# Attention and gated experts on one core: v summed a block early, one fetch moved behind a pair, three casts and one guess moved

## The chip, the core and the metric

The kernel runs on one core of a Trainium2 chip. A core has five engines that run side by side, each through its own instructions in order: TensorE (PE in the rows; PEld is its weight load), VectorE (DVE), ScalarE (ACT), GpSimd (POOL) and SyncE (SP), which here issues transfers. Sixteen DMA engines move data between the device memory (HBM) and the on-chip memory (SBUF). TensorE writes its results into a small accumulator memory (PSUM). The metric is the device time of one execution in microseconds (us).

## The reference

```python
def _attn_ref(q, k, v):                      # q 8x16x384x64, k and v 8x4x384x64
    k = np.repeat(k, group, axis=1); v = np.repeat(v, group, axis=1)
    scores = scale * np.matmul(q, k.transpose(0, 1, 3, 2))
    attn = np.exp(scores - max); attn = attn / attn.sum(-1)
    return np.matmul(attn, v)

def _moe_ref(x, w_group, w_expert, w1, w2):  # x is 3072x1024, 4 groups of 4 experts
    g_idx = argmax(x @ w_group);  g_w = softmax at g_idx
    e_idx = argmax(x @ w_expert[g_idx]);  e_w = softmax at e_idx
    out = g_w * e_w * (relu(x @ w1[g, e]) @ w2[g, e])      # per token, its own expert
```

The output of attention, eight batches of 384 tokens with 1024 features, is the input of the gate and the experts.

## The kernel before, in words

The kernel is one long program in an order written out by hand (`manual_schedule`): each engine gets its instructions in the order of the Python code, and only data and buffers make it wait.

**Attention.** Class `Attn` (line 302) does one batch in 24 units, `run` (line 385): unit u belongs to head group g = u // 6 and to one sixth of the keys. A unit is `score(u + 2)` (four bf16 matmuls into one of two PSUM buffers `ps_s`, line 318, then an exponential on ScalarE, line 324, into a tile `e`), `pv(u)` (four float32 matmuls of v against `e`, line 337, eight instructions in a trace), and `tail(u)`. Scores run two units ahead, so a score waits until the exponential of two units before has emptied its buffer. The sums of the softmax go another way: `pair(u)` adds the `e` of two units on GpSimd (line 345), `reduce(u)` sums the result on VectorE (line 354), where `lags` says at which unit; a unit in `apart` has no pair, and both its tiles are reduced. `join_keys` (line 407) adds up the partial sums of a head group, `sums` (lines 412 to 432) spreads them over the partitions with small matmuls and takes reciprocals on VectorE, and `normalise` (lines 455, 459) transposes these and multiplies the attention output `xT` with them. `cast` (line 464) makes the bf16 copy `xb`.

**Gate and experts.** `gate_logits` (line 474) multiplies `xT` with the gate's weights on TensorE. All tokens of a batch mostly go to the same expert, and the kernel fetches one expert per batch ahead of its use: the gate of the mean of v (a guess) or that of the batch before picks it. `sum_v` adds v's rows up in three instructions on GpSimd (lines 112 to 114), `first_sum_v` does the same in one on VectorE (line 121); `guess_mean` (line 480) and `guess_logits` (line 487) put the sum through the gate on TensorE, and `pick_guess` (lines 568 to 581) turns it into an index with nine small VectorE instructions. `read_pick` (line 558) reads the index on GpSimd, and `pick_w1` and `pick_w2` (lines 546, 552) issue the two weight fetches from GpSimd, 2 MB each as bf16 in SBUF. `after_transposes` (line 604) is a copy of one element that makes GpSimd wait for the DMA transpose of q before it issues them. The expert's product is `moe_h` (line 636, with `xb` as the moving side and `w1`) and `ffn_y` (line 650, with `w2`); `y_out` scales a result and writes it out. If other experts turn out to be needed, a loop behind the main part does them; it didn't run in the profiled execution.

**The order of a batch.** `block(b)` (line 842) stands between the attention of batch b and that of batch b + 1 and does the experts of batch b − 1 together with the normalising and the gate of batch b. TensorE runs `moe_h(f)`, `ffn_y` and `gate_logits` there while the other engines catch up. Batches 0 and 1 have lists of insertions of their own (`steps0`, `steps1`: unit number and what follows it), and so has batch 2 (`first_block` and `steps2`). A tile asked for as "x" takes the PSUM buffer that the running head group doesn't use. Buffers: 16 tiles `e`, two each of v, w1 and w2, one of `xT`, and one of `vsum`.

Of the kernel before, what the change touches and what calls it, by code (L numbers as in the profile page):

```python
# [18 lines left out]
def kernel(  # L19
# [11 lines left out]
    nc = tc.nc  # L31
# [75 lines left out]
    def sum_v(b):  # L107
        t = gpool.tile([P, NA * D], BF16, name="vsum")
# [9 lines left out]
    def first_sum_v():  # L118
        vsum[0] = gpool.tile([P, NA * D], BF16, name="vsum")
        with nc.allow_low_precision(reason="the guess of an expert alone reads this"):  # L120
            nc.vector.tensor_reduce(
                out=vsum[0].rearrange("p (a d) -> p a d", d=D),
                in_=vraw[0].rearrange("p a (c d) -> p a d c", d=D), axis=AX.X, op=ALU.add)
# [288 lines left out]
    def sums(b, g0, g1, which, tiles=False):  # L412
        sm = ps_tile(which)[:, :, :(g1 - g0) * 2 * NB]
        for r in range(2):
# [6 lines left out]
            for t in range(2):  # L421
# [3 lines left out]
                    start=True, stop=True)  # L425
        if b not in inv:
# [3 lines left out]
        for t in range(2):  # L430
            ts = slice(t * D, (t + 1) * D)
            nc.vector.reciprocal(out=iv[ts], in_=sm[ts, :, :, t])  # L432

# [43 lines left out]

    def guess_mean(b, pt):
        pm = pt[:, 1, :2]
        nc.tensor.matmul(out=pm, lhsT=vsum[b], rhs=halfb, start=True, stop=True)  # L480
        vm = gpool.tile([P, 2], BF16, name="vm")
        nc.vector.tensor_copy(out=vm, in_=pm)
        return vm
# [148 lines left out]
    def ffn_h(x, w1, hT, f0, which):  # L632
        h = ps_tile(which)
        for jj in range(2):
            for m in range(KQ):
                nc.tensor.matmul(out=h[:, jj, :S],  # L636
                                 lhsT=w1[:, head_pair(m), (f0 + jj) * P:(f0 + jj + 1) * P],
                                 rhs=x[:, m, :], start=(m == 0), stop=(m == KQ - 1))
# [42 lines left out]
    def before_attention(b):  # L681

        if b + 1 < B:
# [10 lines left out]
             for i in range(5)]  # L694
    at = {
        0: Attn(0, act_copies=(0, 1, 3),
                lags={5: [1], 6: [3], 8: [5], 10: [7], 12: [9], 14: [11], 18: [13], 21: [15],
# [26 lines left out]
    def x_logits(b):  # L724
# [8 lines left out]
        2: [do(first_q1, "x"), first_sum_v],  # L733
# [24 lines left out]
    def first_fetch():  # L758
# [23 lines left out]
            do(at[1].reduce, 7),  # L782
            do(moe_h, 0, 2, "s"),
# [15 lines left out]
    def first_block():  # L799
        load_v(3)  # L800
        moe_y(0, 0, "s")
        sum_v(2)
# [5 lines left out]
        sums(1, 0, Hkv, "o")  # L808
# [7 lines left out]
        at[2] = Attn(2, later=(1,), lags={5: [1], 6: [3], **{u: [u - 2] for u in range(7, NU, 2)}})  # L816
# [25 lines left out]
    def block(b):  # L842
# [12 lines left out]
        else:  # L855
# [3 lines left out]
            if not last:  # L859
                sum_v(b + 1)  # L860
# [213 lines left out]
```

## Time and profile before

| | us |
|---|---|
| median of 3 runs | 357.16 (357.11 to 357.91) |
| profiled execution | 356.7 |
| its span, first to last instruction | 354.9 |
| TensorE busy in the span | 345.9 (97%) |
| VectorE busy | 253.9 (72%) |
| ScalarE busy | 225.0 (63%) |
| GpSimd busy | 220.2 (62%) |
| granted TensorE clock, share of full speed | 0.996 |

The page gives busy time by engine, slices of the span, the chain of work that ended last, and groups of instructions. A timeline lists instructions of one engine in order of time, merged where the same line repeats; in brackets stands the idle time ahead of it and what ended that. Times count from the span's start. A matmul's row shows when it began and a modelled end, so a row can overlap the next one; the distance between starts is the safer reading.

### The profile page before, as it was taken

How to read it: one execution, taken by the hardware profiler on the slowest of the kernel's cores; microseconds unless marked ns; L12 is line 12 of the kernel's file. 1: busy time of each engine (PE TensorE's matmuls, PEld its weight loads, DVE VectorE, ACT ScalarE, POOL GpSimd, SP SyncE). 2: the span in 40 equal slices, each digit the busy share in tenths (PEclk: the TensorE clock that was granted, in tenths of full speed). 3: DMA queues.
4: the chain of work that ended last, by engine and by line, in shares of the span. 5: the costliest groups of instructions: out<-in, count | busy, mean ns of one | idle time of the engine just before them, and what ended most of it. 6: DMA issues, size and time to landing. Idle time of an engine off the chain costs nothing.

```text
span 354.9 us, 9208 instructions
## 1 busy us (share of the span) xinstructions
PE 345.9 (97%) x3801; PEld 182.5 (51%) x3816; DVE 253.9 (72%) x520; ACT 225.0 (63%) x296; POOL 220.2 (62%) x171
## 2 busy tenths in 40 slices
PE   8999999999999999999999999999999999999994
PEld 4455565445555455554555555545545545555642
DVE  5797769767697777976689667886769677796031
ACT  5899925299536795378954499355982669444311
POOL 7889985869935499308991299804995059900000
PEclk9999999999999999999999999999999999999998
DMA  8979999799989999999999999999995995099925
GB/s 199 215 135 188 220 207 160 134 275 222 193 174 176 258 209 182 206 163 203 229 221 207 193 220 211 218 192 193 228 211 95 197 263 130 2 175 219 258 48 137
DMA packets 69327, 67.15 MB, mean 189 GB/s; under 512 B 37113, under 2 KB 49401, under 8 KB 69281
## 3 DMA queue, kind: packets, MB, share of 16 engines
q0 software_dynamic: 26640, 41.03, 67.2%
q1 hardware_dynamic: 42272, 24.94, 30.4%
q8 instruction: 32, 0.52, 0.6%
q10 hardware_dynamic: 368, 0.54, 0.4%
q14 instruction: 15, 0.11, 0.1%
HBM read 86.07 MB, written 12.58 MB: 278 GB/s over the span
## 4 chain that ended last, share of the span: by engine, by line
PE 87%; ACT 4%; POOL 3%; DVE 2%; issue 1%; DMA 1%; ACTq 0%; SPq 0%; POOLq 0%; DVEq 0%
PE ps_o L337 30%; PE ps_s L636 22%; PE ps_s L650 13%; PE ps_s L318 8%; PE ps_o L650 6%; PE ps_o L474 3%; ACT e L324 2%; POOL w L345 2%; PE ps_o L636 1%; PE ps_s L951 1%; PE ps_o L951 1%; DMA w<-in_q_dram 1%; POOL xb L466 1%; ACT w L324 0%; DVE inv L432 0%
## 5 line engine op out<-in xcount | busy, mean ns | idle before, releaser
L345 POOL TENSOR_TENSOR e<-e 128x768 f32<-128x768 f32 x91 | 162.8, 1826 | 37.0 <-PE ps_s L318 30.8
L324 ACT ACTIVATE e<-ps_s 128x768 f32<-128x768 f32 x187 | 147.7, 813 | 15.0 <-PE ps_s L318 12.8
L337 PE MATMUL ps_o<-e,v_raw 64*64 64x384 f32 x1496 | 150.1, 482 | 0.0
L354 DVE TRANSPOSE_TENSOR_REDUCE red<-e 128x24 f32<-128x768 f32 x95 | 91.4, 972 | 36.7 <-POOL e L345 36.6
L636 PE MATMUL ps_s<-xb,w 128*128 128x384 bf16 x480 | 80.1, 326 | 0.1
L337 PEld LDWEIGHTS ps_o<-e,v_raw 64*64 64x64 f32 x1496 | 55.3, 133 | 35.7 <-issue 29.5
L636 PEld LDWEIGHTS <-w 128*128 128x128 bf16 x512 | 49.4, 98 | 36.4 <-issue 4.5
L318 PE MATMUL ps_s<-qT,kT 64*64 64x384 bf16 x768 | 65.0, 325 | 0.4
L650 PEld LDWEIGHTS <-hT 128*128 128x128 bf16 x336 | 31.5, 98 | 37.7 <-issue 1.5
L650 PE MATMUL ps_s<-w,hT 128*128 128x512 bf16 x217 | 49.5, 379 | 0.4
L640 ACT ACTIVATE hT<-ps_s 128x768 bf16<-128x768 f32 x23 | 18.6, 810 | 46.7 <-PE ps_s L636 43.3
L318 PEld LDWEIGHTS <-kT 64*64 64x64 bf16 x768 | 24.5, 105 | 35.6 <-issue 33.6
L669 ACT ACTIVATE ot<-ps_s,we 128x1024 f32<-128x1024 f32 x14 | 15.6, 1115 | 19.0 <-PE ps_s L650 17.2
L604 POOL COPY tok<-qT 1x1 bf16<-1x1 bf16 x6 | 1.1, 179 | 42.5 <-DMA qT<-q_raw 42.5
L379 DVE COPY xT<-ps_o 128x768 f32<-128x768 f32 x26 | 24.0, 924 | 2.7 <-ACT xb L464 1.5
L455 DVE STREAM_TRANSPOSE e<-inv 128x768 f32<-128x768 f32 x26 | 25.2, 971 | 0.2
L464 ACT CAST xb<-xT 128x768 bf16<-128x768 f32 x28 | 23.1, 830 | 3.4 <-DVE xT L459 3.2
L650 PE MATMUL ps_o<-w,hT 128*128 128x512 bf16 x105 | 24.0, 379 | 1.1 <-issue 1.1
L459 DVE TENSOR_TENSOR xT<-xT,e 128x768 f32<-128x768 f32 x24 | 23.1, 962 | 0.8
L495 DVE STREAM_TRANSPOSE gl<-ps_o 128x96 f32<-128x96 f32 x8 | 2.3, 283 | 18.7 <-PE ps_o L474 15.0
L643 ACT ACTIVATE hT<-ps_s 128x384 bf16<-128x384 f32 x14 | 6.1, 488 | 12.5 <-PE ps_o L480 7.2
L474 PEld LDWEIGHTS ps_o<-xT,wg 128*32 128x32 f32 x448 | 9.2, 110 | 3.3 <-issue 2.1
(140 smaller groups left out, 233.3 us busy)
## 6 DMA issues: line engine op xcount, KB each, us to landing
w<-in_moe_w_dram POOLq DMA_DIRECT2D x16, 2048.0 KB, 21.9
out_dram<-ot SPq DMA_DIRECT2D x42, 256.0 KB, 6.9
q_raw<-in_q_dram POOLq DMA_DIRECT2D x7, 768.0 KB, 11.0
v_raw<-in_v_dram SPq DMA_DIRECT2D x7, 384.0 KB, 5.7
k_raw<-in_k_dram POOLq DMA_DIRECT2D x7, 192.0 KB, 6.4
out_dram<-ot SPq DMA_DIRECT2D x10, 128.0 KB, 2.4
w<-in_q_dram POOLq DMA_DIRECT2D x3, 192.0 KB, 6.3
w<-in_k_dram SPq DMA_DIRECT2D x2, 192.0 KB, 3.7
```

Of the source, the lines that this page charges most:

```text
L318: nc.tensor.matmul(out=sT[r * H2:(r + 1) * H2, s, :S], lhsT=kT[b][s * D:(s + 1) * D, key_block(b, s, g // 2, c), ks], rhs=qT[b][s * D:(s + ...
L324: nc.scalar.activation(e.rearrange("p t (s x) -> p s t x", s=2), sT[:, :, :S].rearrange("p s (t x) -> p s t x", t=2), ACT.Exp, scale=scale)
L337: nc.tensor.matmul(out=oT[t * D:(t + 1) * D, r, :S], lhsT=vraw[b][r * H2:(r + 1) * H2, g // 2, c * D:(c + 1) * D], rhs=self.e[u][r * H2:(r ...
L345: nc.gpsimd.tensor_add(out=self.e[u - 1], in0=self.e[u - 1], in1=self.e[u])
L354: nc.vector.tensor_reduce(out=red3[b][:, g, parts[b][g]].rearrange("p t j -> p (t j)"), in_=self.e[w].rearrange("p t (j x) -> p (t j) x", ...
L379: nc.vector.tensor_copy(out=dst, in_=src)
L455: nc.vector.transpose(out=rb.rearrange("p k (j x) -> p k j x", x=32), in_=inv[b][:, ks].unsqueeze(3).to_broadcast([P, 2, NB, 32]))
L459: eng.tensor_mul(out=x, in0=x, in1=rb)
L464: nc.scalar.copy(out=xb[b][:, ks, :], in_=xT[b][:, ks, :])
L474: nc.tensor.matmul(out=pt[32 * t:32 * t + 32, 0, :S // 4], lhsT=wg[:, head_pair(m), :], rhs=x[:, t], start=(m == 0), stop=(m == KQ - 1))
L636: nc.tensor.matmul(out=h[:, jj, :S], lhsT=w1[:, head_pair(m), (f0 + jj) * P:(f0 + jj + 1) * P], rhs=x[:, m, :], start=(m == 0), stop=(m == ...
L650: nc.tensor.matmul(out=y[:, nh, :], lhsT=hT[:, f, c * P:(c + 1) * P], rhs=w2[:, f, nh * HALF:(nh + 1) * HALF], start=(f == 0), stop=(f == ...
```

## The change

Nine edits, all in the order of the work, none in what is computed:

1. `first_sum_v` becomes `reduce_v(b)`, and `vsum` gets two buffers. Batch 2's v is summed by it on VectorE among the insertions behind unit 17 of batch 1; `sum_v(2)` on GpSimd in `first_block` goes.
2. `sums` takes an argument `mean`: the guess matmul of batch 2 stands in the same PSUM tile behind the sums of batch 1, and the copy of its result behind their reciprocals. The insertions of batch 2 lose `x_mean`; `x_logits(2)` moves from behind unit 2 to behind unit 1.
3. Batch 0's sums of head groups 0 and 1 are one call behind unit 19; behind unit 12 none is left. `normalise(0, 0)` moves with it, the join is one call behind unit 16, and the reduction of unit 13 moves from unit 18 to unit 20.
4. Batch 2's first pair is left apart: no addition on GpSimd, two reductions on VectorE behind unit 2; its first head group is joined behind unit 10.
5. The three casts of batch 1's other heads stand together behind the second gate in batch 2's unit 4, not behind units 1, 3 and 6.
6. `ffn_h` runs features 0 to 5 of both halves first where it starts a batch, then features 6 and 7.
7. `block(b)` sums the v of batch b + 2 behind the loads of k and q, not that of batch b + 1. Block 2 sums both.
8. In block 2 the guess matmul of batch 3 comes behind the gate's matmuls, and its logits behind the first two scores of batch 3.
9. The fetch of batch 3's weights moves from block 3 to behind unit 1 of batch 4's attention.

Core of the diff:

```diff
-        t = gpool.tile([P, NA * D], BF16, name="vsum")
+        t = gpool.tile([P, NA * D], BF16, name="vsum", bufs=2)
-    def first_sum_v():
+    def reduce_v(b):
...
-    def sums(b, g0, g1, which, tiles=False):
+    def sums(b, g0, g1, which, tiles=False, mean=None):
+        pt = ps_tile(which)
...
+        if mean is not None:
+            guess_product(mean, pt, MEAN)
...
+        return pt if mean is None else guess_copy(pt, MEAN)
...
+    def guess_product(b, pt, n):
+        nc.tensor.matmul(out=pt[:, 1, n:n + 2], lhsT=vsum[b], rhs=halfb, start=True, stop=True)
+
+    def guess_copy(pt, n):
+        vm = gpool.tile([P, 2], BF16, name="vm")
+        nc.vector.tensor_copy(out=vm, in_=pt[:, 1, n:n + 2])
+        return vm
...
     def ffn_h(x, w1, hT, f0, which):
         h = ps_tile(which)
-        for jj in range(2):
-            for m in range(KQ):
+        ends = [0, KQ] if f0 else [0, KQ - 2, KQ]
+        for m0, m1 in zip(ends, ends[1:]):
+            for jj in range(2):
+                for m in range(m0, m1):
...
-        11: [do(join_keys, 0, 0, 1)],
-        12: [do(sums, 0, 0, 1, "x", True), do(normalise, 0, 0, "x")],
         15: [do(read_pick, 0), do(after_transposes, 1), do(pick_w1, 0), do(pick_w2, 0)],
-        16: [do(join_keys, 0, 1, 2)],
-        19: [do(sums, 0, 1, 2, "x", True)],
+        16: [do(join_keys, 0, 0, 2)],
+        19: [do(sums, 0, 0, 2, "x", True), do(normalise, 0, 0, "x")],
...
             do(at[1].reduce, 7),
+            do(reduce_v, 2),
...
-        sum_v(2)
...
-        sums(1, 0, Hkv, "o")
+        state["vm"] = sums(1, 0, Hkv, "o", mean=2)
...
-        at[2] = Attn(2, later=(1,), lags={5: [1], 6: [3], **{u: [u - 2] for u in range(7, NU, 2)}})
+        at[2] = Attn(2, apart=(1,), lags={6: [3], **{u: [u - 2] for u in range(7, NU, 2)}})
...
-        1: [do(cast, 1, 2), do(at[2].pair, 1), do(x_mean, 2)],
-        2: [do(x_logits, 2)],
-        3: [do(cast, 1, 1)],
-        4.5: [second_gate],
-        6: [do(cast, 1, 3)],
+        1: [second_logits],
+        2: [do(at[2].reduce, 1)],
+        4.5: [second_gate, do(cast, 1, 2), do(cast, 1, 1), do(cast, 1, 3)],
         8: [do(read_pick, 2)],
+        10: [do(join_keys, 2, 0, 1)],
...
+    def fetch(b):
+        if b + 2 < B:
+            after_transposes(b + 2)
+        pick_w1(b)
+        pick_w2(b)
...
             if b + 2 < B:
                 load_k(b + 2)
                 load_q(b + 2)
-            if not last:
-                sum_v(b + 1)
-            if b + 2 < B:
+                sum_v(b + 2)
                 before_attention(b + 1)
-                after_transposes(b + 2)
-            pick_w1(b)
-            pick_w2(b)
+            if b > EARLY:
+                fetch(b)
...
-        elif not last:
-            vm = guess_mean(b + 1, pt)
...
         if not (last or ahead):
-            guess_logits(vm, guess_out(pt))
+            vm = guess_mean(b + 1, pt)
         if b <= EARLY:
             at[b + 1] = Attn(b + 1)
             at[b + 1].start()
+        if not (last or ahead):
+            guess_logits(vm, guess_out(pt))
...
-        return {1: [do(y_out, f, 2, y, True)]}
+        late = [do(y_out, f, 2, y, True)]
+        return {1: late + [do(fetch, b)] if b == EARLY else late}
```

GpSimd between the last loads of block 3 and the pairs of batch 4 stands like this before (lines 546 and 552 are the two weight fetches, 604 the one-element copy, 558 the index that is read, 345 a pair):

```order
L101 DMA q_raw<-in_q_dram 128x8x384
L112 TENSOR_TENSOR vs<-v_raw 128x384
L113 TENSOR_TENSOR vs<-vs 128x2x64
L114 TENSOR_TENSOR vsum<-vs 128x128
L604 COPY tok<-qT 1x1
L546 ISA
L546 DMA w_2149<-in_moe_w_dram 128x8x1024
L552 ISA
L552 DMA w_2151<-in_moe_w_dram 128x8x1024
L558 TENSOR_LOAD e_i
L558 ISA x2
L345 TENSOR_TENSOR e<-e 128x768 x12
```

The same place now (557 and 563 are the fetches, 615 the copy, 569 the index):

```order
L114 TENSOR_TENSOR vsum<-vs 128x128
L569 TENSOR_LOAD e_i
L569 ISA x2
L345 TENSOR_TENSOR e<-e 128x768
L615 COPY tok<-qT 1x1
L557 ISA
L557 DMA w_2442<-in_moe_w_dram 128x8x1024
L563 ISA
L563 DMA w_2444<-in_moe_w_dram 128x8x1024
L345 TENSOR_TENSOR e<-e 128x768 x11
```

The copy and the two fetches stood ahead of all twelve pairs of batch 4 and now stand behind the first of them.

VectorE from the end of batch 0 into batch 1 stands like this before, from the copy of head group 2's output on (432 is a reciprocal, 455 and 459 a normalise, 354 a reduction, 407 a join):

```order
L379 COPY w_307<-ps_o_411 128x768
L354 TENSOR_REDUCE red_305<-e 128x24
L432 RECIPROCAL inv<-ps_o_530 64x24 x2
L354 TENSOR_REDUCE red_305<-e 128x24 x2
L455 STREAM_TRANSPOSE ps_o_597<-inv 128x2x384
L459 TENSOR_TENSOR w_307<-w_307,ps_o_597 128x768
L354 TENSOR_REDUCE red_305<-e 128x24 x2
L379 COPY xT<-ps_o_592 128x768
L354 TENSOR_REDUCE red_305<-e 128x24
L407 TENSOR_REDUCE red<-red_305 128x48
```

And now (435 the reciprocal, 459 and 463 the normalise):

```order
L379 COPY w_307<-ps_o_409 128x768
L435 RECIPROCAL inv<-ps_o_516 64x2x2x12 x2
L459 STREAM_TRANSPOSE ps_o_525<-inv 128x2x384
L463 TENSOR_TENSOR w_307<-w_307,ps_o_525 128x768
L354 TENSOR_REDUCE red_305<-e 128x24 x3
L459 STREAM_TRANSPOSE ps_o_589<-inv 128x2x384
L463 TENSOR_TENSOR w_307<-w_307,ps_o_589 128x768
L354 TENSOR_REDUCE red_305<-e 128x24 x2
L379 COPY xT<-ps_o_584 128x768
L354 TENSOR_REDUCE red_305<-e 128x24
L407 TENSOR_REDUCE red<-red_305 128x48
```

Between the reciprocals and the join that the next sums need there is one normalise more, and the reduction of unit 13 stands behind them now.

ScalarE in batch 2 stands like this before, from the exponential of unit 2 on (324 is an exponential, 464 a cast):

```order
L324 ACTIVATE e<-ps_s_1188 128x2x2x192
L324 ACTIVATE e<-ps_s_1200 128x2x2x192
L464 CAST xb<-xT 128x768
L324 ACTIVATE e<-ps_s_1217 128x2x2x192
L324 ACTIVATE e<-ps_s_1243 128x2x2x192
L464 CAST xb<-xT 128x768
L324 ACTIVATE e<-ps_s_1256 128x2x2x192
L324 ACTIVATE e<-ps_s_1301 128x2x2x192
L324 ACTIVATE e<-ps_s_1317 128x2x2x192
L464 CAST xb<-xT 128x768
```

And now:

```order
L324 ACTIVATE e<-ps_s_1180 128x2x2x192
L324 ACTIVATE e<-ps_s_1192 128x2x2x192
L324 ACTIVATE e<-ps_s_1219 128x2x2x192
L324 ACTIVATE e<-ps_s_1233 128x2x2x192
L324 ACTIVATE e<-ps_s_1245 128x2x2x192
L468 CAST xb<-xT 128x768 x3
L324 ACTIVATE e<-ps_s_1293 128x2x2x192
```

The exponentials of units 2 to 6 run without a cast between them, and three casts stand ahead of that of unit 7.

## Rows read from the trace of the kernel before

**Rows 1.** Page, part 4: chain that ended last, shares of the span

```profile
PE 87%; ACT 4%; POOL 3%; DVE 2%; issue 1%; DMA 1%; ACTq 0%; SPq 0%; POOLq 0%; DVEq 0%
```

**Rows 2.** Timeline (start us, us, engine, line, what, count) of PE, batch 0

```profile
19.23 0.81 PE L337 MATMUL ps_o<-e,v_raw 64*64 64x384 f32 x8
...
20.20 0.30 PE L422 MATMUL ps_o<-red,half 64*64 64x12 f32 x8 [0.15 <-ACT w L377]
...
20.50 0.82 PE L337 MATMUL ps_o<-e,v_raw 64*64 64x384 f32 x8
```

**Rows 3.** Timeline of DVE, end of batch 0 to batch 1

```profile
30.42 0.99 DVE L455 STREAM_TRANSPOSE ps_o<-inv 128x768 f32<-128x768 f32 x1 [0.28 <-ACT w L377]
...
32.32 1.83 DVE L354 TRANSPOSE_TENSOR_REDUCE red<-e 128x24 f32<-128x768 f32 x2
...
36.53 0.32 DVE L407 TENSOR_REDUCE red<-red 128x48 f32<-128x144 f32 x1
...
37.96 0.93 DVE L432 RECIPROCAL inv<-ps_o 64x48 f32<-64x48 f32 x2 [1.12 <-PE ps_o L422]
```

**Rows 4.** Timeline of PE, the two later sums, line 422

```profile
25.99 0.25 PE L422 MATMUL ps_o<-red,half 64*64 64x12 f32 x8
...
37.61 0.28 PE L422 MATMUL ps_o<-red,half 64*64 64x24 f32 x8
```

**Rows 5.** Timeline of PE, first expert block of batch 0

```profile
44.29 3.01 PE L636 MATMUL ps_s<-xb,w 128*128 128x384 bf16 x16
```

**Rows 6.** Chain that ended last (start us, us, what), there

```profile
44.66 0.82 POOL xb L466
...
45.52 1.78 PE ps_s L636 x10
```

**Rows 7.** Timeline of PE, first units of batch 2

```profile
75.12 0.84 PE L337 MATMUL ps_o<-e,v_raw 64*64 64x384 f32 x8
...
78.16 1.53 PE L474 MATMUL ps_o<-xT,wg 128*32 128x96 f32 x64
...
83.29 0.84 PE L337 MATMUL ps_o<-e,v_raw 64*64 64x384 f32 x8
```

**Rows 8.** Timeline of ACT, first units of batch 2

```profile
74.10 1.50 ACT L324 ACTIVATE e<-ps_s 128x768 f32<-128x768 f32 x2
...
75.48 0.84 ACT L464 CAST xb<-xT 128x768 bf16<-128x768 f32 x1
...
81.54 0.82 ACT L464 CAST xb<-xT 128x768 bf16<-128x768 f32 x1
```

**Rows 9.** Timeline of DVE: sum of v, two waits

```profile
11.27 1.52 DVE L121 TENSOR_REDUCE vsum<-v_raw 128x128 bf16<-128x768 f32 x1
...
51.57 0.28 DVE L495 STREAM_TRANSPOSE gl<-ps_o 128x96 f32<-128x96 f32 x1 [1.62 <-PE ps_o L487]
...
77.87 0.23 DVE L581 TENSOR_SCALAR oh_all<-ps_o 128x16 f32<-128x16 f32 x1
```

**Rows 10.** Timeline of POOL, batch 3 to batch 4

```profile
160.14 0.18 POOL L604 COPY tok<-qT 1x1 bf16<-1x1 bf16 x1 [13.58 <-DMA qT<-q_raw]
...
160.74 0.92 POOL L546 DMA_DIRECT2D w<-in_moe_w_dram  x1 [0.42 <-issue]
...
162.81 3.60 POOL L345 TENSOR_TENSOR e<-e 128x768 f32<-128x768 f32 x2 [0.28 <-issue]
```

**Rows 11.** Line 546, first weight fetch of a batch, all eight

```profile
DMA to landing us min/median/max: 13.5/17.5/19.0
```

**Rows 12.** Line 552, second weight fetch of a batch, all eight

```profile
DMA to landing us min/median/max: 24.8/27.7/28.1
```

**Rows 13.** Timeline of PE, batch 4

```profile
161.10 0.81 PE L337 MATMUL ps_o<-e,v_raw 64*64 64x384 f32 x8
...
180.42 10.57 PE L636 MATMUL ps_s<-xb,w 128*128 128x384 bf16 x64
...
190.85 1.46 PE L650 MATMUL ps_s<-w,hT 128*128 128x512 bf16 x5
```

More of the change, by code (lines that the diff above doesn't have):

```diff
@@ L116, in sum_v @@
         vsum[b] = t
-    def first_sum_v():
-        vsum[0] = gpool.tile([P, NA * D], BF16, name="vsum")
+    def reduce_v(b):
+        vsum[b] = gpool.tile([P, NA * D], BF16, name="vsum", bufs=2)
         with nc.allow_low_precision(reason="the guess of an expert alone reads this"):
             nc.vector.tensor_reduce(
-                out=vsum[0].rearrange("p (a d) -> p a d", d=D),
-                in_=vraw[0].rearrange("p a (c d) -> p a d c", d=D), axis=AX.X, op=ALU.add)
+                out=vsum[b].rearrange("p (a d) -> p a d", d=D),
+                in_=vraw[b].rearrange("p a (c d) -> p a d c", d=D), axis=AX.X, op=ALU.add)
     def new_qT(b):
@@ L410, in join_keys @@
                 axis=AX.X, op=ALU.add)
-    def sums(b, g0, g1, which, tiles=False):
-        sm = ps_tile(which)[:, :, :(g1 - g0) * 2 * NB]
+    def sums(b, g0, g1, which, tiles=False, mean=None):
+        pt = ps_tile(which)
+        sm = pt[:, :, :(g1 - g0) * 2 * NB]
         for r in range(2):
@@ L476, in gate_logits @@
                                  start=(m == 0), stop=(m == KQ - 1))
-    def guess_mean(b, pt):
[L479 to L483, printed above, removed]
+    MEAN = 2 * KQ * NB
+    def guess_product(b, pt, n):
[4 more added lines that the diff above has]
+        return vm
+    def guess_mean(b, pt):
+        guess_product(b, pt, 0)
+        return guess_copy(pt, 0)
     def guess_logits(vm, out_):
@@ L633, in ffn_h @@
         h = ps_tile(which)
-        for jj in range(2):
-            for m in range(KQ):
-                nc.tensor.matmul(out=h[:, jj, :S],
-                                 lhsT=w1[:, head_pair(m), (f0 + jj) * P:(f0 + jj + 1) * P],
-                                 rhs=x[:, m, :], start=(m == 0), stop=(m == KQ - 1))
+        ends = [0, KQ] if f0 else [0, KQ - 2, KQ]
+        for m0, m1 in zip(ends, ends[1:]):
+            for jj in range(2):
+                for m in range(m0, m1):
+                    nc.tensor.matmul(out=h[:, jj, :S],
+                                     lhsT=w1[:, head_pair(m), (f0 + jj) * P:(f0 + jj + 1) * P],
+                                     rhs=x[:, m, :], start=(m == 0), stop=(m == KQ - 1))
         if f0 + 2 < FQ:
@@ L696 @@
         0: Attn(0, act_copies=(0, 1, 3),
-                lags={5: [1], 6: [3], 8: [5], 10: [7], 12: [9], 14: [11], 18: [13], 21: [15],
+                lags={5: [1], 6: [3], 8: [5], 10: [7], 12: [9], 14: [11], 20: [13], 21: [15],
                       22: [17]}),
@@ L732 @@
         0: [gate_matrix_2],
-        2: [do(first_q1, "x"), first_sum_v],
+        2: [do(first_q1, "x"), do(reduce_v, 0)],
         4: [do(first_k, NC, 2 * NC, "x")],
@@ L822, in first_block, with second_logits @@
         normalise(1, 3, None, pool)
+    def second_logits():
+        state["pt"] = ps_tile("x")
+        x_logits(2)
     def second_gate():
@@ L858, in block @@
                 load_q(b + 2)
-            if not last:
-                sum_v(b + 1)
-            if b + 2 < B:
+                sum_v(b + 2)
                 before_attention(b + 1)
-                after_transposes(b + 2)
-            pick_w1(b)
-            pick_w2(b)
+            if b > EARLY:
+                fetch(b)
         moe_h(f, 0, "s")
         at[b].reduce(NU - 1)
-        join_keys(b, 0, Hkv)
+        join_keys(b, int(b == 2), Hkv)
         if b == 2:
```

## The prediction

> **What bounds the kernel now.** I read the page's chain of waits first. TensorE is 87% of it and no other engine has over 4% [rows 1], so only two things can shorten the run: instructions taken off TensorE, and the short idle stretches that another engine forces on it. Next I read TensorE's timeline from start to start. A unit of attention takes 0.81 us, the length of its pv row, where nothing interrupts, and I looked for units that take longer. The unit at 19.23 takes 1.27 [rows 2]; the first expert block of batch 0 takes 3.01 for 16 matmuls of which the last ten take 1.78 [rows 5, 6]; the seven units of batch 2 from 75.12 to 83.29 take 8.17 against 7 x 0.81 + 1.53 for the gate between them = 7.20 [rows 7]. Last I read who ends these stretches: ScalarE, VectorE and GpSimd. The changes lie on these three places and on one transfer.
>
> **The parts, one by one.** The profiled execution took 356.7 us, the median of the runs shown is 357.16; the sum is made on 356.7 and 0.46 is added at the end.
>
> *Sums of two head groups in one call (edit 3).* What goes is one insertion: 1.27 − 0.81 = 0.46 us, of which the row charges 0.15 to a wait for ScalarE's copy [rows 2]. That copy stays, and then it delays the scores instead, so between 0.1 and 0.46 goes; I take 0.3. The reciprocals, the normalise and one reduction that stood early now stand on VectorE behind the sums at 25.99. How long until the next join, which the sums at 37.61 need? From the start of the sums to the reciprocals 0.35 (37.61 to 37.96), reciprocals 0.93, normalise 1.90 (30.42 to 32.32), three reductions at 0.92 each 2.75, normalise 1.90, two reductions 1.83, a copy and a reduction taken at the same 0.92 each 1.84, the join 0.32: 11.8 us [rows 3, 4]. TensorE has 37.61 − 25.99 = 11.62 between the two sums [rows 4]. Before, VectorE was idle 1.12 ahead of the reciprocals there [rows 3]; that cover is gone, and TensorE waits about 0.2 for the join, 0.3 with the hand-over. Gain 0.3 less wait 0.3: **0**, between −0.4 and +0.3.
>
> *Order of the first expert matmuls (edit 6).* Ten matmuls take 1.78, 0.16 each with the overlap at the end left out, so the first six should take 0.97; they took 45.52 − 44.29 = 1.23, because the cast on GpSimd ends at 45.48 [rows 5, 6]. With 12 matmuls ahead of the features that this cast writes, TensorE gets there at 44.29 + 12 x 0.16 = 46.2. The wait goes: **−0.25**, at worst nothing. In other batches it only changes an order.
>
> *v of batch 2 on VectorE (edit 1).* The call costs 1.52 us there and stands ahead of an instruction before which VectorE sat idle 1.62 [rows 9]. Covered with 0.1 to spare; without the cover it would delay the gate of batch 0, whose VectorE work TensorE doesn't wait for at once. 0. GpSimd loses three small additions in a stretch where it waits anyway: 0.
>
> *Guess, casts and pair of batch 2 (edits 2, 4, 5).* Of the 0.97 lost from 75.12 to 83.29, ScalarE explains most: a cast of 0.84 stands between exponentials of 0.75 (two take 1.50), at 75.48, once more two exponentials later, and at 81.54 [rows 8], and scores wait for buffers. The second gate at 78.16 also waits for the last instruction of the index, 77.87 + 0.23 = 78.10 [rows 7, 9]. After the change: the result copy of the guess stands on VectorE behind the reciprocals and ahead of the normalise that the first cast waits for. It shifts that cast and the exponentials behind it by some 0.2, so that unit 2 starts at 75.3, not 75.12. From there three units run at 0.81, to the end of unit 4 at 77.7. The logits have moved up by a unit, so the index is done about 1.1 earlier than 78.10 and the gate need not wait. It takes 1.53, to 79.3. Three casts together take 3 x 0.75 = 2.25 beside it, 0.7 longer than the gate; the two score buffers hold all but 0.2 of that. Units 5 to 8 end at 79.3 + 4 x 0.81 + 0.2 = 82.7 where they ended at 83.29. **−0.55**; with none of the ScalarE waits gone 0, with the rest of the 0.97 gone too −0.9. The pair that is left apart takes 1.8 us off GpSimd, and two reductions of 0.92 stand on VectorE where the next gate result is over 1 us away; neither is what TensorE waits for: 0.
>
> *Guess of batch 3 in block 2 (edit 8).* The same matmuls in another place. The logits now wait for the copy behind the guess, with eight score matmuls between them as cover; the trace has no such sequence. At least 0, at most the 0.3 that an insertion between scores costs above. I take **+0.05**, nearer the covered end.
>
> *v a block ahead (edit 7).* The sum may now wait on GpSimd for the load of v. Behind it stands only the one-element copy, before which GpSimd sat idle 13.58 us [rows 10]. In block 6 the fetch comes some 2 us earlier, which nobody waits for. 0.
>
> *Fetch of batch 3 behind a pair (edit 9).* This is the part that can cost. The fetch was issued at 160.74, as soon as the transposes had landed [rows 10]. Now the pair of unit 1 stands ahead. It needs the pv that starts at 161.10 and ends at 161.91 [rows 13], runs 1.8 (3.60 for two, rows 10) and is over at 163.8 to 163.9: the fetch is 3.15 us later against TensorE's work. The second weight tile is issued 0.92 behind, at 164.8, and TensorE wants it at 190.85 [rows 10, 13]. The eight of the trace landed 24.8 to 28.1 after their issue [rows 12], that is at 189.6 to 192.9: a wait between 0 and 2.05. The median, 27.7, gives 1.65; but those fetches share the DMA engines with output writes, of which more are gone when this one starts, so I take the middle, 26.45, landing at 191.27: **+0.4**. The first tile, 17.5 behind 163.9, comes at 181.4 against 180.42 [rows 11, 13]; with the same saving it is on time, and a wait there would be part of the other, not on top. The first pair starts 0.8 earlier than at 162.81, the other eleven about 1.1 later, and only sums at the batch's end hang on them.
>
> The notes have a price for such a fetch. By the Trainium skill, "DMA: Bandwidth & Descriptors", section "Anatomy of one DMA — SWDGE (gpsimd) path", a transfer from GpSimd's queue takes about 2.0 us plus its bytes at 436 GB/s. As an estimate from that page, two tiles of 4 MB in float32 would take 21 us, the second would land near 185, and the sum would be −0.75 in all. The trace disagrees: no second tile landed in under 24.8 us [rows 12].
>
> Sum: 0 − 0.25 − 0.55 + 0.05 + 0.4 = −0.35 on 356.7; at the median 357.16 − 0.35 = **356.8**.
>
> **Rivals.** *The fetch is in time.* If the second tile takes no more than 26.05 us from issue, nothing waits: −0.75, 356.4. For it: one of eight took 24.8. Against it: the median.
>
> *The fetch is late.* One mechanism, in block 4: above 26.05 us every tenth is TensorE's. At 27.7 the sum is −0.75 + 1.65 = +0.9, 358.1; at 28.1 +1.3, 358.5. From 26.8 on the kernel is slower than before. For it: most of the eight lie there. Against it: the outputs that leave earlier.
>
> *The small waits give more.* If the join is in time and ScalarE was the only cause in batch 2: −0.4 − 0.25 − 0.9 = −1.55 with the fetch in time, 355.6. Against it: the 1.12 of cover is spent by my own sum.
>
> *It doesn't do what it says*: the parts cancel exactly. That is inside the forecast's range.
>
> **How the numbers follow.** A difference of 0.3%, 1.07 us, is about what a measurement of this kernel can tell from none. Forecast 0.32, fetch in time 0.26, more from the small waits 0.20, fetch late 0.22. Faster by over 0.3% (under 356.1): 0.18 of the third and 0.04 of the second, 0.22. Slower (over 358.2): 0.15, the late part of the fourth. Within: 0.63. The range reaches from the third case at 355.6 to between the two prices of the fourth, 358.3; the forecast's own is 356.3 to 357.5.
>
> **What would show it.** Right: no insertion at unit 12 of batch 0, but a gap of some 0.3 before the sums of batch 1's unit 9, with VectorE's idle time there gone; no gap in the first 16 matmuls of the expert; units 2 to 8 of batch 2 in about 7.4 us; the weights of batch 3 issued some 3 us later against batch 4's first pv, and a gap of some tenths in TensorE before the first product with w2 in block 4. Wrong: no gap there, or one of over 1 us; a gap at the logits of batch 3; or any change of the other fetches' waits, since I price all later blocks at nothing.

## The result and the profile after

The changed kernel takes **360.26 us** (median of nine runs, 357.95 to 361.64) where before takes 357.2 (nine runs, 356.72 to 357.98). The ratio is 1.0071, 95% interval [1.0042, 1.0100]: slower, by 0.7%. All ratios are to before on the same chip and leave out disturbed runs, so that they need not be the quotient of two medians. The forecast was 356.8 with a range to 358.3. The profiled execution took 358.38, with a span of 356.5 us.

The chain that ended last has lost TensorE's share to transfers (shares of the span, to set beside [rows 1]):

```profile
PE 84%; DMA 9%; ACT 3%; DVE 1%; issue 1%; ACTq 0%; DVEq 0%; POOLq 0%
```

TensorE's timeline of after (start us, us, engine, line, what, count, idle time and what ended it), first up to batch 2, answering [rows 2, 4, 5, 7], then in batch 4, answering [rows 13]:

```profile
19.54 0.81 PE L337 MATMUL ps_o<-e,v_raw 64*64 64x384 f32 x8
...
20.35 0.82 PE L337 MATMUL ps_o<-e,v_raw 64*64 64x384 f32 x8
...
21.38 0.84 PE L337 MATMUL ps_o<-e,v_raw 64*64 64x384 f32 x8
...
26.06 0.28 PE L423 MATMUL ps_o<-red,half 64*64 64x24 f32 x8
...
37.71 0.31 PE L423 MATMUL ps_o<-red,half 64*64 64x24 f32 x8
...
44.42 2.77 PE L649 MATMUL ps_s<-xb,w 128*128 128x384 bf16 x16
...
75.16 0.84 PE L337 MATMUL ps_o<-e,v_raw 64*64 64x384 f32 x8
...
77.54 1.53 PE L478 MATMUL ps_o<-xT,wg 128*32 128x96 f32 x64
...
82.60 0.84 PE L337 MATMUL ps_o<-e,v_raw 64*64 64x384 f32 x8
...
160.13 0.81 PE L337 MATMUL ps_o<-e,v_raw 64*64 64x384 f32 x8
...
180.38 10.57 PE L649 MATMUL ps_s<-xb,w 128*128 128x384 bf16 x64 [0.86 <-DMA w<-in_moe_w_dram]
...
192.43 1.90 PE L663 MATMUL ps_s<-w,hT 128*128 128x512 bf16 x8 [1.47 <-DMA w<-in_moe_w_dram]
```

Up to batch 4 the change does what it says. Its first pv comes at 160.13, 0.97 us ahead of before [rows 13], though this execution's loads let TensorE into unit 12 of batch 0 0.31 later (19.54 against 19.23). Then TensorE waits 0.86 + 1.47 = 2.33 us for batch 3's two weight tiles, and is behind. So the question is why these weights are late. GpSimd's timeline shows when each transfer was asked for. Of before, as far as it was not shown, and of after, answering [rows 10]:

```profile
104.45 0.94 POOL L546 DMA_DIRECT2D w<-in_moe_w_dram  x1 [0.42 <-issue]
...
141.31 0.74 POOL L96 DMA_DIRECT2D k_raw<-in_k_dram  x1
143.54 0.89 POOL L101 DMA_DIRECT2D q_raw<-in_q_dram  x1 [1.50 <-DMA qT<-q_raw]
```

```profile
106.10 0.94 POOL L557 DMA_DIRECT2D w<-in_moe_w_dram  x1 [0.42 <-issue]
...
141.18 0.74 POOL L96 DMA_DIRECT2D k_raw<-in_k_dram  x1 [0.79 <-DMA kT<-k_raw]
146.89 0.89 POOL L101 DMA_DIRECT2D q_raw<-in_q_dram  x1 [4.98 <-DMA qT<-q_raw]
...
162.88 0.18 POOL L615 COPY tok<-qT 1x1 bf16<-1x1 bf16 x1
163.00 0.91 POOL L557 DMA_DIRECT2D w<-in_moe_w_dram  x1
163.91 0.88 POOL L563 DMA_DIRECT2D w<-in_moe_w_dram  x1
```

The lateness starts with transposes that land at 105.45, some 74 us ahead of TensorE's first wait, which begins at 180.38 − 0.86 = 179.52. Each step waits for the one above it; the load of q of batch 5 makes up 1.4 on the way, in 9.6 us instead of 11.1:

| us | before | after | later by |
|---|---|---|---|
| transposes of batch 3: issued | 98.29 | 98.25 | 0 |
| landed | 103.80 | 105.45 | 1.65 |
| weights of batch 2: issued | 104.45 | 106.10 | 1.65 |
| transposes of batch 4: issued, as q lands | 137.41 | 138.96 | 1.55 |
| landed | 142.98 | 146.33 | 3.35 |
| q of batch 5: load issued | 143.54 | 146.89 | 3.35 |
| transposes of batch 5: landed | 160.09 | 162.00 | 1.91 |
| weights of batch 3: issued | 160.74 | 163.00 | 2.26 |
| second tile landed | 189.35 | 192.39 | 3.04 |

Two steps add most of it: the transposes of batch 3 and of batch 4 take 7.2 and 7.4 us to land instead of 5.5 and 5.6. Of before and of after, the view of the DMA queues in the stretch in which each was issued (line, queue, count, median us to landing):

```profile
qT<-q_raw SPq DMA_TRANSPOSE x1, 5.5
...
qT<-q_raw SPq DMA_TRANSPOSE x1, 5.6
```

```profile
qT<-q_raw SPq DMA_TRANSPOSE x1, 7.2
...
qT<-q_raw SPq DMA_TRANSPOSE x1, 7.4
```

What else was on the queues? The packets of the transposes of batch 3 end by 103.4 in both kernels. In after, the 1.1 us behind that, 103.35 to 104.45, hold this (queue, kind: packets, MB, share of 16 engines):

```profile
q1 hardware_dynamic: 130, 0.18, 64.7%
q8 instruction: 1, 0.02, 5.5%
q14 instruction: 1, 0.01, 1.8%
```

q8 carries program code in blocks of 16 KB, 32 in either run, q14 in blocks of 8 KB. One block occupied one DMA engine for 5.5% x 16 x 1.1 = 0.97 us, between the end of the transposes' packets and their landing. In before no such block lies there: the same two blocks pass at 104.8 and 105.0, 1.5 us behind. At the second step, in after, it is the load of k of batch 5, issued at 141.18, 2.2 us behind the transposes: 143.9 to 146.1 holds 135 of its packets (q0), and 146.33 is when the transposes land. In before the same load was issued at 141.31, 3.9 us behind them, and they landed after 5.6. So far this is what the traces show side by side; the experiments test it.

```profile
q0 software_dynamic: 135, 0.10, 70.8%
q1 hardware_dynamic: 81, 0.17, 22.1%
```

### The profile page after: what moved, and what is told of

Same layout as the page of the kernel before. It is cut to its first block, busy times and chain, and to the rows that moved or that the text cites. A ratio compares the mean times of both kernels' runs of the same rounds, so it can differ in the third digit from the quotient of the medians.

```text
span 356.5 us, 9200 instructions
## 1 busy us (share of the span) xinstructions
PE 346.8 (97%) x3808; PEld 183.0 (51%) x3808; DVE 257.1 (72%) x520; ACT 225.1 (63%) x296; POOL 217.3 (61%) x167
## 4 chain that ended last, share of the span: by engine, by line
PE 84%; DMA 9%; ACT 3%; DVE 1%; issue 1%; ACTq 0%; DVEq 0%; POOLq 0%
PE ps_o L337 29%; PE ps_s L649 19%; PE ps_s L663 13%; PE ps_s L318 8%; DMA w<-in_moe_w_dram 8%; PE ps_o L663 6%; PE ps_o L478 3%; ACT e L324 2%; PE ps_o L649 1%; PE ps_s L970 1%; DMA w<-in_moe_w_expert_dram 1%; PE ps_o L970 1%; ACT w L324 0%; DVE inv L435 0%; ACT ot L682 0%
## 5 line engine op out<-in xcount | busy, mean ns | idle before, releaser
L345 POOL TENSOR_TENSOR e<-e 128x768 f32<-128x768 f32 x90 | 160.9, 1820 | 39.3 <-PE ps_s L318 38.5
L663 PE MATMUL ps_o<-w,hT 128*128 128x512 bf16 x112 | 25.5, 380 | 0.0
L459 DVE STREAM_TRANSPOSE e<-inv 128x768 f32<-128x768 f32 x26 | 25.2, 971 | 0.2
L112 POOL TENSOR_TENSOR vs<-v_raw 128x384 f32<-128x384 f32 x6 | 6.8, 1135 | 6.7 <-DMA v_raw<-in_v_dram 6.7
```

What stands on the lines that cost most here:

```text
L345: nc.gpsimd.tensor_add(out=self.e[u - 1], in0=self.e[u - 1], in1=self.e[u])
L459: nc.vector.transpose(out=rb.rearrange("p k (j x) -> p k j x", x=32), in_=inv[b][:, ks].unsqueeze(3).to_broadcast([P, 2, NB, 32]))
L663: nc.tensor.matmul(out=y[:, nh, :], lhsT=hT[:, f, c * P:(c + 1) * P], rhs=w2[:, f, nh * HALF:(nh + 1) * HALF], start=(f == 0), stop=(f == ...
```

## The experiments

Thirteen kernels were run. They stand here by the question that they answer.

**Is it the place of the fetch?** Theory A: the late fetch is the whole loss. B: the chain of transfers. C: the sum of v a block ahead holds up GpSimd. D, in the later runs, is B made exact: the transposes land late because another transfer, program code or the load of k, is served at the end of their data.

After with the fetch of batch 3 back in block 3 (e1):

```
-            if b > EARLY:
-                fetch(b)
+            fetch(b)
...
-        return {1: late + [do(fetch, b)] if b == EARLY else late}
+        return {1: late}
```

> The changed kernel with edit 9 alone undone: batch 3's weights are fetched in block 3 again, ahead of all pairs of batch 4. Theory A (the late fetch): the other edits gain about 1.2 us, and the whole loss is the fetch behind the pair, 2.4 us of TensorE waiting for w in block 4 in the profiled run. Then 357.2 - 1.2 = 356.0, and no wait for w over 0.3 us. Theory B (the chain of transfers): the fetch can't be issued before the transposes land anyway, so whatever TensorE gains before batch 4 is given back in block 4: 357.0 to 357.5, with a wait for w of about 1 us left. Theory C (the sum of v a block ahead holds up GpSimd and the loads): as the changed kernel, about 360.

1.0088 [1.0056, 1.0121]: no better. The times of A and B are missed, that of C comes out. Nothing waits for weights, but TensorE stands 4.90 us in batch 4:

```profile
175.16 1.56 PE L337 MATMUL ps_o<-e,v_raw 64*64 64x384 f32 x8 [4.90 <-DVE xT L379]
```

On GpSimd the one-element copy ahead of the fetch waited 14.07 us for transposes that landed at 167.0 (7.2 us, once more with a code block on their end), with the pairs of batch 4 queued behind it; VectorE's reductions waited for the pairs. The row's 1.56 us is the second price of the wait: the granted clock is 0.50, the level of 1.2 GHz, from 175 to 178 us, and the three units from 175.16 took 4.64 us (to 179.80) instead of 2.42. Before with the later fetch alone (e2):

```
-            pick_w1(b)
-            pick_w2(b)
+            if b > EARLY:
+                pick_w1(b)
+                pick_w2(b)
...
+        if b == EARLY:
+            late += [do(after_transposes, b + 2), do(pick_w1, b), do(pick_w2, b)]
```

> The kernel before with edit 9 alone: batch 3's weights are fetched behind unit 1 of batch 4. The second tile then is issued some 3 us later than at 161.65 and was 1.5 us early. Theory A: a wait of 1.5 to 2.2 us for w in block 4, 358.9 to 359.4. Theory B: the same. Theory C: 357.2, no wait.

0.9995 [0.9984, 1.0006]: it costs nothing, and A and B are missed again, since the fetch was issued at 164.50 and landed in 15.0 and 25.2 us, the second tile at 190.58. After with the fetch behind unit 3 (e4, `3: [do(fetch, b)]` in place of unit 1):

> The changed kernel with the fetch behind unit 3 of batch 4, so behind one more pair: issued 1.8 us later. Theory A: every tenth is TensorE's, the wait for w in block 4 grows by 1.8 us, the fastest runs go from 358 to about 359.8. The runs of the changed kernel spread from 357.95 to 361.64: if what comes ahead of the fetch (transposes that land late) makes that spread, GpSimd's pairs now decide when it is issued and the runs lie within 1 us; if the transfer itself makes it, they spread as wide, to about 363.

1.0103 [1.0068, 1.0138], waits of 1.8 and 1.2 us for weights: 0.7 more than in after, not 1.8, and the runs spread at least as wide, over 4.3 us. Theory A falls: in after the place of the fetch moves the time little, and undoing it brings nothing back. Theory C still stands here.

**Which half of the change?** Before with the edits on GpSimd and its loads alone (g3: 1, 7 and 9), and after with edits 7 and 9 undone (g4). The core of g3's edit, which g4 turns round:

```
-                load_q(b + 2)
-            if not last:
-                sum_v(b + 1)
+                load_q(b + 2)
+                sum_v(b + 2)
```

> The kernel before with the edits on GpSimd and its loads alone: sum of v of batch 2 by VectorE, of each later batch a block ahead, batch 3's weights fetched behind a pair of its attention. TensorE's order is that of before. Theory C: 359 to 361. Theory D: TensorE is not ahead, so its code load misses batch 3's transposes (landing after 5.5 us) and the time is that of before, 357.0 to 357.5.

> The changed kernel with the sum of v back in its old block (for batches 4 to 7) and batch 3's weights fetched in block 3 as before: the edits on TensorE and ScalarE and batch 2's sum on VectorE alone remain. Theory C: 356.0 to 356.4. Theory D: TensorE is 1 us ahead, the code load hits batch 3's transposes (7.2 us), and the chain is late by 3 us: 358.5 to 361.

g3: 1.0015 [1.0002, 1.0028], transposes of batch 3 at 5.5; its 358.22 us is a little over D's 357.5 and far from C's 359 to 361. g4: 1.0097 [1.0073, 1.0122], transposes at 6.5 and 7.3; TensorE waits for the mean of v, whose sum on GpSimd stood behind the late load of q. Theory C falls, and the loss comes with the edits that make TensorE earlier.

**Is it the code?** The kernel before, with 28 warm-up products instead of 9 (g2; 3584 columns instead of 3840, so hardly the "same columns" of the text below, but no more of them):

```
-        for i, n in enumerate((4, 4, 4, 4, 4, 4, 4, 1, 1)):
+        for i, n in enumerate((1,) * 28):
```

> The kernel before with nothing changed but its warm-up: the same columns in 28 products of 128 columns instead of 9 of up to 512, so some 38 more instructions in TensorE's program and none of the edits. Its tenth 16 KB load of program code, at 104.8 us before and 1.5 us behind the end of the data of batch 3's transposes, is asked for about 1.6 us earlier. Theory D: it falls on the end of those transposes, which land 7.2 us after their issue instead of 5.5; the weights of batches 2 and 3 come 1.5 to 3 us later, and the time is 357.5 to 359.5 (before has 1.5 to 2 us of slack there). If code loads have nothing to do with it: 357.2, transposes at 5.5.

1.0078 [1.0054, 1.0101], 360.29 us: as slow as the changed kernel, with none of its edits, and slower than D's 357.5 to 359.5. TensorE is not early in it: its first pv of batch 3 comes at 119.31, in before at 118.96. The tenth code block now passes at 103.4, the transposes of batch 3 take 7.1 and those of batch 4, with the load of k, 7.4. Of this kernel, GpSimd's loads and TensorE's mean of v:

```profile
106.11 0.94 POOL L546 DMA_DIRECT2D w<-in_moe_w_dram  x1 [0.42 <-issue]
...
147.11 0.89 POOL L101 DMA_DIRECT2D q_raw<-in_q_dram  x1 [4.71 <-DMA qT<-q_raw]
...
150.24 0.45 POOL L114 TENSOR_TENSOR vsum<-vs 128x128 bf16<-128x128 f32 x1
```

```profile
150.75 0.18 PE L480 MATMUL ps_o<-halfb,vsum 128*128 128x2 bf16 x1 [1.88 <-DVE e L455]
```

These issue times are those of after to within 0.3 us. The 1.88 us is put down to VectorE, but the product's other input, the sum on GpSimd, ended at 150.24 + 0.45 = 150.69, 0.06 ahead of it; the weight load of the same product is charged 2.3 us to that sum. That is the wait that edit 7 takes away in after, where the chain is paid for at the weights instead.

The reverse, less code in after, was tried twice: five warm-up products instead of nine and the sums of batch 0 as two products a call (h1, 16 instructions fewer), and the sums alone (j1, 8 fewer).

```
...
-        19: [do(sums, 0, 0, 2, "x", True), do(normalise, 0, 0, "x")],
+        19: [do(sums, 0, 0, 2, "x"), do(normalise, 0, 0, "x")],
...
-        9: [do(sums, 0, 2, Hkv, "x", True)],
+        9: [do(sums, 0, 2, Hkv, "x")],
```

> The changed kernel with 16 instructions fewer on TensorE ahead of batch 2 and every edit kept: five warm-up products instead of nine, and the sums of batch 0 as two products of 48 columns a call instead of four of 24. It is the reverse of adding code to the kernel before: TensorE's tenth 16 KB code load is asked for some 0.7 us later. Theory D: if that takes it past the end of the data of batch 3's transposes (103.3 us), they land after 5.5 us, the weights of batch 2 come 1.7 us earlier, the next load of k no longer gets into batch 4's transposes, and the time falls from 360.3 to 356.3 to 358; if the load still falls within the transposes, 360 as before, and nothing is learnt. Rival (code loads only go along with the loss): transposes at 5.5 us and still 360.

> The changed kernel with its warm-up as it was and 8 instructions fewer on TensorE: the sums of batch 0 as two products of 48 columns a call instead of four of 24. The run with 16 fewer took the 16 KB code load past batch 3's transposes (10.3 us behind their issue), but its shorter warm-up left TensorE 4.1 us late at the start, so its time tells nothing. Theory D: with the 16 KB load past them the transposes land after 5.5 to 6.5 us (6.5 where the 8 KB code load of another engine still falls on their end, as it did there), and the time is 357.0 to 359.5; if 8 instructions are too few to move it, 7.2 us and 360. Rival (code loads only go along with the loss): 5.5 to 6.5 us and still 360.

h1: 1.0092 [1.0065, 1.0119]; j1: 1.0090 [1.0069, 1.0111]. In both the 16 KB block moved past the transposes, but the 8 KB one did not, and they took 6.5 and 6.6. TensorE also fell behind earlier on: its last pv ahead of the first expert block came 4.1 and 1.4 us later than in after. So the first step gave back only 0.7 us, and the load of k met the transposes of batch 4 all the same (7.1 and 7.3). Taken by its words, j1 came out as its rival had it (6.5 and still 360). With TensorE late and the second step still there, neither run decides it: that taking the code block away brings the time back is not shown.

**Is it the load of k?** After with block 3's load of k held until the transposes of batch 4 have landed (j2):

```
+                if b == EARLY:
+                    after_transposes(b + 1)
                 load_k(b + 2)
```

> The changed kernel with a one-element copy on GpSimd ahead of block 3's load of k, so that this load is asked for only when batch 4's transposes have landed. Theory D, second link (a load asked for while transposes run is served ahead of their completion): batch 4's transposes land after 5.5 us instead of 7.4, the loads of k and q are asked for within 1 us of each other at 145 to 146, q lands at 155 to 156.5 instead of 156.5, batch 3's weights up to 1.5 us earlier: 358.8 to 360. If the load of k has no part in it: 7.4 us, and 360 to 361 since k starts later.

1.0027 [1.0011, 1.0042], 358.65 us. The transposes of batch 4 land after 5.5 although those of batch 3 still take 7.2, and the waits for weights, 0.86 + 1.47 = 2.33 in after, are 1.50 together:

```profile
180.96 10.57 PE L649 MATMUL ps_s<-xb,w 128*128 128x384 bf16 x64 [1.03 <-DMA w<-in_moe_w_dram]
...
192.00 2.33 PE L663 MATMUL ps_s<-w,hT 128*128 128x512 bf16 x10 [0.47 <-DMA w<-in_moe_w_dram]
```

So by the runs the second step is worth some 0.0071 − 0.0027 = 0.44% of the time, 1.6 us, a little more than half the loss. What is left looks different. The transposes of batch 5 landed at 161.16, but the fetch still came 2.88 us behind batch 4's first pv (160.54), as in after (2.87), because now the pair holds it:

```profile
161.53 1.82 POOL L345 TENSOR_TENSOR e<-e 128x768 f32<-128x768 f32 x1 [9.29 <-PE ps_s L318]
163.30 0.18 POOL L615 COPY tok<-qT 1x1 bf16<-1x1 bf16 x1
163.42 0.92 POOL L557 DMA_DIRECT2D w<-in_moe_w_dram  x1
```

That is edit 9. So it seems that it is not free once TensorE is early; j2 without it was not run.

**What takes the chain off the end?** First by not waiting: after without the copies that hold the fetches behind the transposes (g1).

```
     def fetch(b):
-        if b + 2 < B:
-            after_transposes(b + 2)
         pick_w1(b)
...
-            after_transposes(b + 1)
             pick_w1(b)
```

> The changed kernel without the one-element copy on GpSimd by which the weight fetches of batches 2 to 5 wait until the transposes ahead of them have landed. Theory D (the loss sits in the chain of transfers: transposes, weights, q, transposes, weights; the transposes' completion comes 7.2 to 7.4 us after their issue instead of 5.5 because another transfer asked for meanwhile is served at the end of their data, ahead of their last completion write, and everything behind waits): the chain no longer waits for that completion, w1 of batch 2 lands at 121 or earlier instead of 124.2, w2 of batch 3 before 188, TensorE does not wait for weights, time 356.0 to 356.8. Theory C (the sums of v a block ahead hold up GpSimd and the loads behind them): the sums are as they were, time stays 359 to 361. A third way, the fetches now compete with the transposes and make them land so late that the scores of the next batch wait: over 361.

1.0584 [1.0557, 1.0611]. The third way came true: the fetches run first and the transposes finish behind them.

```profile
127.35 0.86 PE L318 MATMUL ps_s<-qT,kT 64*64 64x384 bf16 x8 [13.35 <-DMA qT<-q_raw]
```

Then by order: the weights of a batch ahead of the next k and q. In block 3 alone (e3, `EARLY = 4`) and in blocks 3 to 5 (h2, `EARLY = 6`) of after, and in blocks 3 to 5 of before (h4):

```
-    EARLY = 3
+    EARLY = 6
...
-            sum_v(b + 1)
+            if b == 2:
+                sum_v(b + 1)
...
-            if b > EARLY:
-                fetch(b)
+            fetch(b)
...
-        return {1: late + [do(fetch, b)] if b == EARLY else late}
+        return {1: late}
```

This is h2's edit; e3 has 4 for the 6, and in h4 the number alone changes. With it edit 9 is gone, and edit 8's place for the logits holds in more blocks.

> The changed kernel with block 3 in the order of block 2: its weights are fetched as soon as the transposes of batch 4 have landed, near 143 to 146, ahead of the loads of k and q of batch 5, and batch 5's first two scores stand in block 4. Theories A and B: no wait for w in block 4 and the gains of the other edits stay, less some 0.4 us for the two scores that are no longer hidden: 356.0 to 356.6, runs within 1 us of one another. If instead the loads of batch 5, now behind the weights, come too late, a wait at the start of batch 5. Theory C: 359 to 360.

> The changed kernel with every block up to block 5 in block 2's order: a batch's weights are fetched ahead of the next k and q, so that in no block two loads of k and q and two sets of transposes stand between one fetch and the next. Theory D: transposes may still land after 7.2 us, but each fetch then has 5 us or more to spare, no wait for weights or for a late GpSimd is left, TensorE keeps its 1 us: 355.9 to 356.5. If the loss has another source on TensorE: 357.2 or more.

> The kernel before with the same order of fetches and loads in blocks 3 to 5 and none of the edits. Theory D: before has no wait for weights to lose, so 357.0 to 357.4; the difference to the changed kernel in that order (356.2) is what the edits on TensorE are worth, 0.8 to 1.1 us. Rival (the order of the fetches is itself a gain): under 356.7.

| | order of before | weights always first |
|---|---|---|
| without the edits | 1 | 1.0002 [0.9981, 1.0023] |
| with them | 1.0071 [1.0042, 1.0100] | **0.9964 [0.9949, 0.9979]** |

e3, with block 3 alone, is between them: 0.9999 [0.9983, 1.0015], 357.19 us where 356.0 to 356.6 was expected. h2 takes 356.59 us and beats both kernels; h4 takes 358.04, over the 357.0 to 357.4 expected, on a chip where before takes 357.72. In h2 the transposes of batch 3 still take 7.2 us with the code block on their end, and cost nothing: the first weights of batch 3 are issued at 145.74 instead of 163.00, and TensorE goes through block 4 without a wait.

```profile
160.51 0.81 PE L337 MATMUL ps_o<-e,v_raw 64*64 64x384 f32 x8
...
179.50 10.57 PE L649 MATMUL ps_s<-xb,w 128*128 128x384 bf16 x64
189.94 5.34 PE L663 MATMUL ps_s<-w,hT 128*128 128x512 bf16 x23
...
202.64 0.81 PE L337 MATMUL ps_o<-e,v_raw 64*64 64x384 f32 x8
```

The same edits, but for edit 9, are worth −0.4% where the chain has time to spare, and all nine +0.7% where it has none. This table, and not a single wait, is what the cause rests on. It shows that the loss needs the old order of the transfers; it does not part the two steps.

## Why the prediction was wrong, point by point

*Sums of two groups in one call: 0.* The insertion at unit 12 is gone. The wait for ScalarE moved into the next unit (20.35 to 21.38, 1.03 instead of 0.81), as the prediction said it might; the unit with the sums at 37.71 in it takes 0.95 (37.06 to 38.01), so that the wait for the join is nearly nothing: the join was done at 37.65, 11.59 behind the first sums at 26.06, where the prediction counted 11.8. From unit 12 to the first expert block 25.06 us became 24.88: −0.18, within its bounds.

*First expert matmuls: −0.25.* 3.01 became 2.77: −0.24. Right.

*Guess, casts and pair of batch 2: −0.55.* The stretch took 82.60 − 75.16 = 7.44 where 7.4 was forecast and 8.17 was before. It is −0.73 against its own first unit, which the prediction expected 0.2 late. It is 0.15 late: the expert's block ended 0.11 us ahead of before (47.19 against 47.30), and this unit starts 0.04 behind (75.16 against 75.12). So the term came to −0.58. Right, with its parts.

*Guess of batch 3 in block 2: +0.05.* Nothing waits there.

Together TensorE is 0.97 ahead at batch 4, 1.28 with the late start taken out, where the terms gave 0.75: 0.28 more came in block 2, which the prediction priced at nothing (0.69 ahead at 82.60, 0.97 at 160.13), and 0.18 from the sums. This half was right and a little modest, and h2 against h4 bears it out (356.59 and 358.04).

*Fetch of batch 3 behind a pair: +0.4.* **This is the step that failed**: "The fetch was issued at 160.74, as soon as the transposes had landed. Now the pair of unit 1 stands ahead." It took all that comes before the fetch as it was, and it took too short a time to landing (below): a wait of 0.4 was forecast, 0.86 + 1.47 = 2.33 was measured. The fetch did come about as much later against batch 4's first pv as forecast (2.87 behind it instead of 0.36 ahead, 3.23; forecast 3.15), but for another reason. The transposes landed at 162.00, 1.91 later than before, and the pair, done at 162.95, added some 0.3. With the first pv 0.97 earlier, the fetch would have been 2.9 later against it without edit 9. So the agreement was chance, and e1 and e2 bear it out: the edit undone gains nothing, the edit alone costs nothing. The rival "the fetch is late" gave 358.1 to 358.5, and the profiled execution took 358.38 by that very wait. Its mechanism, the pair ahead of the fetch, added 0.3 in after; in j2, where the transposes of batch 4 land on time, it is what holds the fetch.

*The second tile lands 26.45 after its issue.* It took 28.47 (192.39 − 163.91). This is the term that was mis-sized, by 2.0 us. The price put on it held: above 26.05 us every tenth is TensorE's, which makes 2.42 of 28.47, against the 2.33 measured, and 1.58 of j2's 27.63, against 1.50. The saving taken for output writes that would be gone did not come: two outputs were issued at 163.46 and 164.20, beside it. In e2, with the fetch 1.5 later, it was 25.2. That the outputs make this difference was not tested. The eight of after, to set beside [rows 12], are as wide as before:

```profile
DMA to landing us min/median/max: 24.7/27.4/28.5
```

*"I price all later blocks at nothing"* and the same for earlier transfers: the text named "any change of the other fetches' waits" as what would make it wrong, and so it was. What was missing from the working was one line: the slack of the chain. In the trace of before the two tiles landed at 178.28 and 189.35 for wants at 180.42 and 190.85 [rows 13], 2.1 and 1.5 us to spare. An edit that makes TensorE 1 us earlier uses up most of that by itself.

What stays open: the profiled execution of after lost 2.33 us in waits, but the median of its runs is 1.9 us slower than it. The profiles of e1, g2, g4 and j1 pay for the same late chain at three different places (4.9 us at VectorE's copy; 1.9 at the mean of v and 0.6 at weights; 2.2 at the mean; 1.8 and 1.5 at weights), so it may be that other executions pay more; none of them was profiled. The granted clock points the same way. Behind a long wait it falls (e1 above; in g4, 0.58 and 0.57 from 151 to 155 us, behind the 2.2 us wait), and its mean is 0.992 or 0.993 in four of the five slowest executions of after, where none of the 79 executions of before in the experiments is under 0.994.

Why the code block passes so near the transposes' end is shown in part. g2 shows that moving TensorE's instructions moves it; the instruction that calls for it was not found. But it need not be called for at just that moment. In the fifteen traces 55 blocks of 16 KB start within 5.3 us of the issue of q's transposes (batches 2 to 7): 16 in the first 1.5 us, 4 in the next 3.4, and 35 between 4.97 and 5.28, where the transposes' packets end. So it seems that most blocks called for while these packets run wait for their end; when a block was called for is not in the traces.

## What to carry to other kernels

Before an edit makes the bounding engine faster, write down for each transfer how long it lands before it is wanted; that slack, not the engine's own row, is the bound of the gain. Where transfers run in a chain that takes nearly a whole period, look for the place where two loads come between two fetches, and change the order there first. And more instructions in TensorE's program alone can move the time by as much as the edit under study (0.78% in g2), so a control with more instructions and none of the edits is worth a run.

## What the runs showed of the hardware

- A transfer that is served at the end of DMA transposes can hold up their completion. With nothing there the transposes of q land in 5.5 us; with an 8 KB code block alone in 6.5 (h1) and 6.6 (j1); with a 16 KB block that starts 4.97 to 5.28 us behind their issue in 7.0 to 7.3 (32 of 35), but in 6.5 once (g4, batch 3) and in 5.5 for batch 6 of before and of e1, which landed while the block ran. With the load of k it is 7.1 to 7.4. The kernel before has one such landing itself, 7.15 for batch 2, where nothing waits for it. The Trainium skill, "DMA: Bandwidth & Descriptors", section "Queues, rings and completion order", says that a completion write lands only behind every earlier write of the same DMA engine, across its queues. The trace agrees as far as it goes: the block, from 103.43 to 104.40, lies between the end of the data (103.43) and the landing (105.45); a packet's DMA engine is not in the trace. Its 0.97 us is a part of the 1.65 us that were lost; the rest is not explained.
- 38 instructions more in the warm-up, with no more columns, cost 0.78% [0.54, 1.01] (g2). The waits in its profile are those of a late chain of transfers: 1.88 us at the mean of v and 0.6 at weights.
- Behind a wait of TensorE the granted clock fell to 0.50, 1.2 GHz, and the work behind the wait took longer: 2.2 us more over three units in e1 (wait 4.90), and in g4 (wait 2.24) 7.03 us for 24 products with w2 that take 5.34 in after.
- Two fetches, 4 MB as written, that were issued ahead of transposes (97.23 and 98.16, the transposes at 98.57) left them unfinished for 28.65 us, and the scores waited 13.35 us (g1). A one-element copy that waits for the transposes, which looks like idle time on GpSimd, is what prevents it.
- With five warm-up products instead of nine (h1), the products of batch 0 between 8 and 14 us took 0.84 us instead of the 0.48 of after, and TensorE ended batch 1's attention 4.1 us later. The granted clock is shown as 1.00, the level of 2.4 GHz, in that stretch of both runs. But 0.84 us is also what the same products take behind e1's wait, where 0.50 is shown, so here the length of the products tells more than that column.
